# Chunk 1 of a Mamba-2 scan in two half-length units, and weight pieces joined one step later

## The chip, the cores and the metric

The kernel runs on one core of one Trainium2 chip. The metric is the device time of one execution in microseconds (us). The three runs of the kernel before gave 376.62, 376.66 and 376.97 us; their median, 376.66 us, is the time that the change is measured against. The profiled execution, from which all other times here come, spans 374.1 us.

## The reference, cut to what matters

```python
# batch 4, heads 8, sequence 768, head_dim 32, d_state 16; all float32
for c in range(nc):                                  # per head; state is [16, 32]
    cum = np.cumsum(log(clip(a[c])))                 # decay within the chunk
    L   = np.exp(cum[:, None] - cum[None, :]) * causal
    M   = (C @ B.T) * L
    y   = M @ x + (C @ state) * np.exp(cum)[:, None]
    state = exp(sum(la)) * state + (B * decay_to_end).T @ x
# then, with the heads side by side as 256 features, for 3072 tokens:
h = y @ w_in            # 256 -> 2048
g = h * np.cos(h)
out = g @ w_out         # 2048 -> 256
```

The result does not depend on the chunk length; the kernel chooses its own.

## The kernel before, in words

**Order of the work.** The sequence of 768 tokens is cut into six chunks of 128 tokens (`NC` = 6), for all four sequences together, so one chunk is 512 tokens. The feed-forward part of a chunk takes 16 steps (`NF` = 16), numbered through the whole kernel: steps 0 to 15 are chunk 0, 16 to 31 chunk 1, and so on up to 95. A step n consists of these parts, each on its engine, and each engine takes its instructions in the order in which the program writes them:

- `first(n)`, TensorE: eight matmuls (L668) make `hp`, 256 features of h for half of the chunk's tokens, in PSUM. `hp` has two banks, so `first(n)` needs the bank that step n-2 used.
- `wind(n)`: ScalarE makes k from `hp` (L675), VectorE makes w (L681).
- `gate(n)`: ScalarE takes the cosine (L690). `gated(n)`: VectorE multiplies `hp` with it into `gT` (L695), which frees the bank.
- `second(n-2)`, TensorE, two steps later (`LAG` = 2): `gT` times `w_out`. In chunk 0 that is eight matmuls of L739; from chunk 1 on it is a seven-product form (`seven`, L777), for which GpSimd prepares sums of `gT` in `differ` (L720 to L723) and sums of weights in `differ_w` (L714, in steps 14, 15, 17 and 19).

In chunk 0 a step takes the tokens of one *unit*: 64 tokens of every sequence (`turn_of`: even steps unit 0, odd steps unit 1, each two steps on the same 256 features). In the later chunks a step takes all 128 tokens of two sequences.

**Weights in pieces.** The weights come in as double words and have to be rounded to float32 on the chip. Each of `w_in` and `w_out` has eight pieces; piece j of either holds what the steps 2j and 2j+1 of a chunk use. `fetch` starts the load, `grade` takes the absolute value on ScalarE (L231), clips it on GpSimd (L232) and prepares the last bit on ScalarE (L229), and `join` builds the word on VectorE (L244, then L246) and adds the last bit on GpSimd (L254). `piece` (L886) says which piece belongs to which step: `out` j to step 2j, `in` j to step 2j-3. In the loop, step n grades the piece of step n+1 and joins the piece of step n; `join` stands after `wind(n)` and ahead of `gated(n)` in VectorE's queue. Pieces fetched but not joined hold one of eight `words` buffers.

**The scan.** Chunk 0 is scanned as two units of 64 tokens (`inner`, `weights`, `finish0`), with its decays spread over partitions by matmuls (`spread_a`) and scanned on VectorE by `decays0`. Chunk 1 is scanned as the later chunks are, one pair of sequences (u = 0, 1) at a time: `decays` scans a row of decays of 128 tokens of four heads (L515), eight times per chunk; `reaches` scans the decay from the chunk's start (L506); `turn2` turns B and C (for chunk 1 by four TensorE transposes, L543, later by VectorE, L529); `intra2` makes C times B (L565); `masked` multiplies it with the decays (L586, eight VectorE instructions per pair); `finish2` makes y and the state (L600, L607, L628) and `carry` sums the state (L640 on VectorE, L644 on GpSimd). `plan` (L892 to L899) says in which step which of it stands: for chunk 1, pair 0, the decays in steps 4, 6, 8 and 9, `turn2` in 11, `intra2` in 12 and `finish2` in 14; pair 1 in 14 to 17, 18, 19 and 21. VectorE does the decays behind `gated(n)` as long as there are pieces.

**Loads.** `rest_of_loads` (L906) writes the order of SyncE's DMA queue: chunk 1's data, sequence by sequence, between the remaining weight pieces.

Of the kernel before, what the change touches and what calls it, by code (L numbers as in the profile page):

```python
# [25 lines left out]
def kernel(  # L26
# [17 lines left out]
    P = 128  # L44
# [46 lines left out]
    def load(c, seqs=(0, NB), only=(B, C, x)):  # L91

        if c >= NC:
            return
        if c not in raw:
            raw[c] = (loads.tile([P, 2, NB * H, N], FP32, tag="bc", name="bc"),
                      loads.tile([P, NB, H, D], FP32, tag="xr", name="xr"))
        bc, xr = raw[c]
        xr = xr.rearrange("p b h d -> p (b h) d")
        for dst, src in ((bc[:, 0], B), (bc[:, 1], C), (xr, x))[::2 if c > 1 else 1]:  # L100

            if not any(src is o for o in only):
                continue
            halves = src is not C
            for b in range(*seqs) if halves else seqs[:1]:
                rs = slice(b * H, (b + 1 if halves else seqs[1]) * H)
                for t in range(2 if halves and b % 2 else 1):
                    n = W if halves and b % 2 else P
                    ts = slice((n - t * W) % P, (n - t * W) % P + n)
                    nc.sync.dma_start(  # L110
                        out=dst[ts, rs], in_=src[b:b + 1 if halves else seqs[1], :,
                                                 c * P + t * W:c * P + t * W + n, :]
                        .rearrange("b h s n -> s (b h) n"))
# [3 lines left out]
    both = loads.tile([P, 2, NB * H, N], FP32, tag="bc", name="bc")  # L117
    bs = both[:, 0].rearrange("p (k q h) n -> p k q (h n)", k=2, q=2)
    c4 = both[:, 1].rearrange("p (h r) n -> p h r n", h=H)
    xrs = {}  # L120

    def load_b(k, s, eng=nc.sync):

        eng.dma_start(out=bs[s * W:(s + 1) * W, k].rearrange("p q (h n) -> p (q h) n", h=H),
                      in_=B[2 * s:2 * s + 2, :, k * W:(k + 1) * W, :]
                      .rearrange("b h i n -> i (b h) n"))
# [7 lines left out]
    def load_x(k, s, eng=nc.sync):  # L134
        if k not in xrs:
            both = loads.tile([P, 2, 2, H, D], FP32, tag="xr", name="xr")
            xrs.update({i: both[:, i] for i in range(2)})
        eng.dma_start(out=xrs[k][s * W:(s + 1) * W].rearrange("p q h d -> p (q h) d"),
                      in_=x[2 * s:2 * s + 2, :, k * W:(k + 1) * W, :]
                      .rearrange("b h i d -> i (b h) d"))  # L140

    def by_blocks(c, u):
        return c > 1
# [22 lines left out]

    def load_along(c, seqs=range(NB)):

        if c >= NC:
            return  # L170
        if c not in along:
            along[c] = rows.tile([P, NB, P], FP32, tag="along", bufs=2, name="along")
        for b in seqs:
            nc.sync.dma_start(
                out=along[c][:, b], in_=a_all[b, :, c * P:(c + 1) * P].unsqueeze(1)
                .to_broadcast([H, N, P]))
# [8 lines left out]
                            .rearrange("p (b i) -> p b i", b=NB) for i in range(3))  # L185
    a_in = const.tile([RB, NU, P], FP32, name="a_in")
# [168 lines left out]
    def decays0(k, p, i=0, n=1):  # L355

        if p == i == 0:
            lams[k] = scan.tile([P, 2, H, W], FP32, tag="lam", bufs=4, name="lam")
        flat = "p h i -> p (h i)"
        hs = slice(i * H // n, (i + 1) * H // n)  # L360
        V.tensor_tensor_scan(out=lams[k][:, p, hs].rearrange(flat),
                             data0=spread.pop((k, p, i)).rearrange(flat),
                             data1=unit0[:, hs].rearrange(flat), initial=0.0,
                             op0=ALU.mult, op1=ALU.add)

    def weigh0(k):
        scs[k] = sc = scan.tile([P, 2 * H, N], FP32, tag="sc0", bufs=1, name="sc0")
        G.tensor_tensor(out=sc, in0=bs[:, k].rearrange("p q (h n) -> p (q h) n", h=H),
                        in1=lams[k].rearrange("p q h i -> p (q h) i")[:, :, W - 1:W]
                        .to_broadcast([P, 2 * H, N]), op=ALU.mult)  # L370
# [4 lines left out]
    bTs = scan.tile([P, 2, 2, P], FP32, tag="turned", bufs=1, name="turned0")  # L375
# [16 lines left out]
    def turn_b(k, tp):  # L392

        for p in range(2):
            PE.transpose(tp[:, 2 * k + p], bs[:, k, p], ident)
        return lambda: ACT.copy(out=bTs[:, k], in_=tp[:, 2 * k:2 * k + 2])
# [15 lines left out]

    def inner(k, t):

        gs[k, t] = g = pair("g")
        bT, cT = bTs[:, k], cuts[k]
        for p, s, q in ((p, s, q) for p in range(2) for s in range(2) for q in range(2)):
            ss, q_ = slice(s * W, (s + 1) * W), 2 * t + q
            r = slice(32 * q_, 32 * q_ + 32)
            PE.matmul(g[ss, q, p * P:(p + 1) * P].rearrange("p (t i) -> p t i", t=2),  # L420
                      lhsT=bT[r, p, ss], rhs=cT[r, :, p, ss], start=True, stop=True,
                      tile_position=(32 * q_, s * W), skip_group_check=True)

    def weights(k, q):

        m_of[k] = units[k]
        m, l = (ap[:, :, HH * q:HH * (q + 1)].rearrange("p s (k t) i -> p k s (t i)", k=2)
                for ap in (units[k], lams[k]))
# [3 lines left out]
    def finish0(k):  # L432

        m, xk = units[k], xrs[k]
# [31 lines left out]
        if k == 0:  # L466
            yT[0] = two.tile([P, 2, 2, 2 * P], FP32, tag="yT", name="yT")
        t_ = yT[0][:, k]
# [15 lines left out]
        def add():  # L484
            dec = scan.tile([P, 2, 2, 2 * D], FP32, tag="whole", bufs=1, name="whole")
            r4 = reach1.rearrange("p (q s) i -> p s q i", s=2)
# [4 lines left out]
            for u in range(2):  # L491
                state[0, u] = new[:, u].rearrange("p s (t d) -> p s t d", t=2)
# [40 lines left out]
    def turn2(c, u):  # L533
        bc = raw[c][0]

        if by_blocks(c, u):
            tp = turned.pop((c, u)).rearrange("p k s i -> p s k i")
            bT = tp[:, :, 0]
        else:
            tp = pair("tp")[:, 0].rearrange("p (s k i) -> p s k i", s=2, k=2)  # L540
            for s in range(2):
                for k in range(2):
                    PE.transpose(tp[:, s, k],  # L543
                                 bc[:, k, heads(2 * u + s)].rearrange("p h n -> p (h n)"), ident)
            bT = scan.tile([P, 2, 2, P], FP32, tag="turned", bufs=1, name="bT2")[:, 0]
            ACT.copy(out=bT, in_=tp[:, :, 0])
# [24 lines left out]
    def masked(c, b):  # L571
# [5 lines left out]
        if c == 1:  # L577
# [77 lines left out]
    def first(n, between=None, tag="h"):  # L655
# [4 lines left out]
        if c == 0:  # L660
            to_, y = hp[n].rearrange("p (e i) -> p e i", e=2), yT[0][:, u]
# [87 lines left out]
    def seven(n):  # L749
# [39 lines left out]
        def rest():  # L789
# [6 lines left out]
            for s in range(2):  # L796
                nc.sync.dma_start(out=to_rows[2 * u + s, c],
# [79 lines left out]
    def clips():  # L877
# [3 lines left out]
        for dst, src in ((a_cut, cut), (a_all, la)):  # L881
# [10 lines left out]
    late = [((0,), {0: 11}, [(4, 0, 0), (6, 0, 1), (8, 1, 0), (9, 1, 1)], 14),  # L892
            ((1,), {1: NF + 2}, [(NF - 2 + i, 2 + i // 2, i % 2) for i in range(4)], NF + 5)]
# [4 lines left out]
    plan = [(c, NF * (c - 1), *v) for c in range(1, NC) for v in (  # L898
        late if c == 1 else [(*at_once[:2], halves_of.get(c, each), at_once[2])])]  # L899

    def chunk1(b):
        load(1, (b, b + 1))
        load_along(1, (b,))
        load_a(1, (b,))

    def rest_of_loads():  # L906
        for w in (0, ("out", 3), ("in", 5), ("out", 4), 1,
                  ("in", 6), ("out", 5), ("in", 7), 2, ("out", 6), ("out", 7), 3):
            chunk1(w) if isinstance(w, int) else fetch(*w)
# [15 lines left out]
    def ends(n):  # L925
# [3 lines left out]
    block_loads = {NF * (c - 1) - 9 + 8 * u: (c, u) for c in range(2, NC) for u in range(2)  # L929
                   if by_blocks(c, u)}  # L930
# [3 lines left out]
    def first_steps():  # L934
# [3 lines left out]
        units_of_decay()  # L938
# [38 lines left out]
        join("in", 3)  # L977
        gated(3)
        grade("out", 2)
        return add_s1  # L980

    add_s1 = first_steps()
    rest_of_loads()
    for n in range(AHEAD, NC * NF + LAG):
        c, f = divmod(n, NF)
        if n < NC * NF:

            if c > 0 and f == (NJ if c == 1 else 0):
                if c == 1:
                    load(2, only=(x,))  # L990
                load(c + 2)
            first(n)
# [3 lines left out]
            rests = []  # L996
            if n + 1 in piece:
                rests.append(grade(*piece[n + 1], later=True))
            gate(n)
            for rest in rests:  # L1000
                if rest:
                    rest()
            if n in piece:
                join(*piece[n])

            behind = [lambda at=at: halved(*at) for at in halves_at(n)]
            behind = [lambda at=(c, 2 * u + 1): masked(*at) for c, u in pairs(n - 2)] + behind
            if n not in piece and behind:
                behind.pop(0)()
            gated(n)  # L1010
            if n == AHEAD + 2:
                add_s1()
            for do in (*behind, *unsummed):
                do()
            unsummed.clear()
        for i, js in differ_at.get(n, ()):
# [3 lines left out]
        for c, u in pairs(n - 1):  # L1020
            intra2(c, u)
            masked(c, 2 * u)
        for c, us in ends(n):
# [3 lines left out]
        for c, u in pairs(n + 1):  # L1027
# [3 lines left out]
            if by_blocks(c, u):  # L1031
                turn_blocks(c, u)
# [36 lines left out]
```

## Time and profile before

| what | us |
|---|---|
| median of three runs | 376.66 |
| span of the profiled execution | 374.1 |
| TensorE busy | 364.3 (97%) |
| VectorE busy | 282.7 (76%) |
| GpSimd busy | 216.1 (58%) |
| ScalarE busy | 172.1 (46%) |
| `hp` of step 4 starts | 27.16 |
| `hp` of step 24 starts | 106.67 |
| chunk 1's eight scans (L515), one each | 1.92, 1.92, 1.91, 1.92, 1.98, 1.22, 2.05, 1.42 |

In the page, a group is a line, an engine, an operation and its tiles with their shapes, then the number of instructions, the busy time and the mean of one. In a timeline, a line starts with the start and the duration of an instruction or of a merged run of them, and ends in brackets with the time for which the engine stood idle before it and what ended that. TensorE's granted clock is 1.0 throughout. A TensorE instruction of float32 counts twice in the profile (eight matmuls of `first(n)` for the four in the code). TensorE's busy share is no measure of its pace, since matmuls overlap: the distance between the starts of `hp` in two steps is.

### The profile page before, as it was taken

To read this page: it belongs to the slowest core of one execution; us is meant where nothing else is said; L and a number is where in the kernel's file an instruction comes from. 1 tells how busy PE (TensorE), PEld (TensorE's weight loads), DVE (VectorE), ACT (ScalarE), POOL (GpSimd) and SP (SyncE) were. 2 spreads that over 40 slices of the span, in tenths; PEclk is the share of its full clock that TensorE was granted. 3 is DMA by queue.
4 is the path that set the end of the run, shared out by engine and by line. 5 is a ranking of instruction groups with operands and counts; after the bars stand their busy time and mean duration, and the time that the engine had idled before them with its cause. 6 is when DMAs were issued, how large, how long until landed. Compare 5 with 4: busy or idle time off the path is not lost.

```text
span 374.1 us, 8667 instructions
## 1 busy us (share of the span) xinstructions
PE 364.3 (97%) x3262; PEld 326.9 (87%) x3262; DVE 282.7 (76%) x473; ACT 172.1 (46%) x293; POOL 216.1 (58%) x334
## 2 busy tenths in 40 slices
PE   8998999999999999999999999999999999999996
PEld 5687777889899899999899998999999989999995
DVE  7788999989699957987867987766887872554543
ACT  3586756444344434354434435434444443443442
POOL 6667765589946346665454693453785344544451
PEclk9999999999999999999999999999999999999999
DMA  9969797514545742653222745221020000010011
GB/s 147 283 180 257 206 255 127 128 14 97 140 106 76 133 95 31 88 151 93 59 54 22 133 99 135 28 45 17 3 41 8 13 18 2 2 28 0 2 31 29
DMA packets 121354, 31.55 MB, mean 84 GB/s; under 512 B 90496, under 2 KB 117216, under 8 KB 121312
## 3 DMA queue, kind: packets, MB, share of 16 engines
q1 hardware_dynamic: 119024, 30.54, 38.3%
q10 hardware_dynamic: 2288, 0.46, 0.7%
q8 instruction: 26, 0.43, 0.5%
q14 instruction: 16, 0.13, 0.1%
HBM read 27.64 MB, written 3.34 MB: 83 GB/s over the span
## 4 chain that ended last, share of the span: by engine, by line
PE 64%; DVE 13%; SPq 7%; POOL 7%; issue 4%; ACT 2%; DMA 2%; DVEq 0%; POOLq 0%; ACTq 0%
PE hp L668 30%; PE o L777 25%; SPq L155 4%; POOL words L714 3%; DVE gT L695 2%; DVE w L681 2%; PE y L607 2%; SPq L110 2%; DVE mag L246 2%; DVE lam L515 2%; DVE mag L244 2%; DMA arow<-a_cut 1%; PE y L600 1%; PE g L565 1%; PE a_ps L351 1%
## 5 line engine op out<-in xcount | busy, mean ns | idle before, releaser
L668 PE MATMUL hp<-yT,w_in 128*128 128x256 f32 x768 | 183.5, 382 | 3.2 <-DVE gT L695 2.9
L668 PEld LDWEIGHTS hp<-yT,w_in 128*128 128x128 f32 x768 | 139.3, 190 | 23.8 <-issue 5.7
L720 POOL TENSOR_TENSOR gd<-gT 128x256 f32<-128x256 f32 x79 | 59.0, 747 | 99.1 <-DVE gT L695 97.2
L690 ACT ACTIVATE w<-w,quarter 128x512 f32<-128x512 f32 x96 | 69.2, 721 | 80.2 <-DVE w L681 80.1
L681 DVE SCALAR_TENSOR_TENSOR w<-hp,k 128x512 f32<-128x512 f32 x96 | 65.5, 682 | 40.4 <-ACT k L675 40.2
L675 ACT ACTIVATE k<-hp 128x512 int32<-128x512 f32 x96 | 57.1, 595 | 79.7 <-PE hp L668 79.5
L695 DVE TENSOR_TENSOR gT<-hp,w 128x512 f32<-128x512 f32 x96 | 65.2, 680 | 33.2 <-ACT w L690 24.3
L777 PE MATMUL o<-words,gd 128*128 128x128 f32 x474 | 65.9, 275 | 0.0
L777 PEld LDWEIGHTS o<-words,gd 128*128 128x128 f32 x474 | 59.3, 192 | 0.0
L515 DVE TENSOR_TENSOR_SCAN lam<-arow,unit 128x512 f32<-128x512 f32 x40 | 56.5, 1411 | 0.0
L777 PEld LDWEIGHTS o<-w_out,gT 128*128 128x128 f32 x316 | 47.6, 191 | 3.9
L723 POOL TENSOR_TENSOR gd<-gT,gd 128x128 f32<-128x128 f32 x79 | 44.6, 565 | 6.2
L777 PE MATMUL o<-w_out,gT 128*128 128x128 f32 x316 | 48.0, 275 | 0.0
L722 POOL TENSOR_TENSOR gd<-gT,gd 128x128 f32<-128x128 f32 x79 | 44.1, 558 | 6.2
L586 DVE TENSOR_TENSOR m<-g,lam 128x256 f32<-128x256 f32 x80 | 30.9, 414 | 0.5
L739 PE MATMUL o<-w_out,gT 128*128 128x256 f32 x128 | 30.2, 380 | 0.4 <-POOL w_out L254 0.4
L777 PE MATMUL o<-w_out,gd 128*128 128x128 f32 x158 | 30.6, 275 | 0.0
L777 PE MATMUL o<-words,gT 128*128 128x128 f32 x158 | 30.6, 275 | 0.0
L739 PEld LDWEIGHTS o<-w_out,gT 128*128 128x128 f32 x128 | 24.2, 190 | 4.0 <-POOL w_out L254 0.8
L777 PEld LDWEIGHTS o<-words,gT 128*128 128x128 f32 x158 | 24.0, 192 | 0.0
L777 PEld LDWEIGHTS o<-w_out,gd 128*128 128x128 f32 x158 | 24.0, 192 | 0.0
L794 DVE TENSOR_TENSOR sum<-ps,sum 128x256 f32<-128x256 f32 (+1 forms) x27 | 16.7, 644 | 0.6
(109 smaller groups left out, 269.5 us busy)
## 6 DMA issues: line engine op xcount, KB each, us to landing
arow<-a_cut SPq DMA_DIRECT2D x20, 512.0 KB
words<-in_moe_w_in_dram SPq DMA_DIRECT2D x8, 512.0 KB
words<-in_moe_w_out_dram SPq DMA_DIRECT2D x8, 512.0 KB
out_dram<-sum SPq DMA_DIRECT2D x18, 128.0 KB
blocks<-in_B_dram SPq DMA_DIRECT2D x128, 8.0 KB
blocks<-in_C_dram SPq DMA_DIRECT2D x128, 8.0 KB
xr<-in_x_dram SPq DMA_DIRECT2D x14, 128.0 KB
along<-a_all SPq DMA_DIRECT2D x20, 64.0 KB
```

The source lines that it names most:

```text
L515: V.tensor_tensor_scan(out=lam[c, b][:, hs].rearrange("p h i -> p (h i)"), data0=rows_.rearrange("p h i -> p (h i)"), data1=unit[:, b % 2 ...
L586: V.tensor_tensor(out=m_[js, :, :, is_], in0=g_[js, :, :, is_], in1=l_[js, :, :, is_], op=ALU.mult)
L668: PE.matmul(to_[:, e], lhsT=w_in[:, k, fs], rhs=y[:, k], start=(k == 0), stop=(k == KT - 1), skip_group_check=True)
L675: ACT.activation(k, hp[n], AF.Copy, bias=0.25, scale=INV_2PI)
L681: V.scalar_tensor_tensor(out=w, in0=hp[n], scalar=INV_2PI, in1=k, op0=ALU.mult, op1=ALU.subtract)
L690: ACT.activation(cos, cos, AF.Sin, bias=quarter, scale=TWO_PI)
L695: V.tensor_tensor(out=gT[n], in0=hp.pop(n), in1=cos, op=ALU.mult)
L720: G.tensor_tensor(out=d[:, 0:2], in0=g[:, 1:2].to_broadcast([P, 2, P]), in1=g[:, 3::-3], op=ALU.subtract)
L722: G.tensor_tensor(out=d[:, 2], in0=g[:, 0], in1=d[:, 0], op=ALU.subtract)
L723: G.tensor_tensor(out=d[:, 3], in0=g[:, 2], in1=d[:, 2], op=ALU.subtract)
L739: PE.matmul(o[c, u][:, t], lhsT=g[:, 2 * e + t], rhs=w_out[:, 2 * j + e], start=(j == e == t == 0), stop=(j == NJ - 1 and e == 1), skip_gr ...
L777: PE.matmul(at[q], lhsT=a_[q], rhs=w[q], start=(j == 0 and q in starts), stop=(j == NJ - 1), skip_group_check=True)
```

## The change

Chunk 1 is scanned as chunk 0 is: in two units, here numbered k = 2 and 3, each 64 tokens of all four sequences. It is for less work on VectorE: a scan of 64-token rows covers twice as many (sequence, head) pairs per instruction, and half of a 128x128 causal square is not computed at all. The second part moves `join` one step behind `grade`, so that a piece's clip lies a whole step ahead of the join.

```diff
-        if by_blocks(c, u):
-            ...
-        else:
-            tp = pair("tp")[:, 0].rearrange("p (s k i) -> p s k i", s=2, k=2)
-            ...
-                    PE.transpose(tp[:, s, k], ...)
+    def load_arow(k):            # two loads of [W, 2H, W] per unit
+    def load_unit_along(k):      # four loads of [H*N, W] per unit
...
+    def reach_unit(k):           # one VectorE scan of 128x260
+    def turn_unit(k):            # 4 transposes, ACT: bT, 2 x cT; VectorE: rT
...
-            if n + 1 in piece:
-                rests.append(grade(*piece[n + 1], later=True))
+            rest = grade(*piece[n], later=True) if n in piece else None
             gate(n)
...
-            if n in piece:
-                join(*piece[n])
+            joins = n - 1 in piece and piece[n - 1] in held
+            if joins:
+                join(*piece[n - 1])
...
+    unit_at = {2: ((6, 8), 9, 11, 12, 14),
+               3: ((NF - 1, NF), NF + 1, NF + 2, NF + 3, NF + 5)}
...
         gate(3)
         rest()
         second(1)
-        join("in", 3)
         gated(3)
-        grade("out", 2)
...
-        if c == 1:
+        if c == 2:
 
             G.memset(m[W - s * W:P - s * W, :, 0:W], 0.0)
```

`unit_at` gives for each unit the steps of the two decay scans (`decays0`), of `reach_unit`, of `turn_unit`, of `inner` with the first half of `weights` (the second half follows a step later), and of `finish0`; the state's sum (`add`, three GpSimd instructions, L488 and L490) follows a step after `finish0`. `units_of_decay`, two GpSimd copies (L873, L875), moves from the first steps to the end of step 16, behind `weigh0(3)`. The memsets of the mask tiles (L579) move from chunk 1 to chunk 2. `rest_of_loads` is written anew in the order of the units, with chunk 2's first rows of decays loaded in steps 12 and 17; the shapes of `first`, `seven` and the output of chunk 1 follow the units.

## The prediction

> **What bounds the kernel now.** I read the page's busy shares first, then the busy time in stretches of 10 us, then the timelines of TensorE and VectorE through chunk 0, where the change acts. The stretches (sums of busy time of PE, PEld, DVE, ACT, POOL in us) show two regimes:
>
> ```profile
> 40.00:50.00 10.00, 9.82 (x46) 8.36 (x45) 9.90 (x13) 7.29 (x13) 8.62 (x11) 1.00 0.91 249
> 50.00:60.00 10.00, 9.29 (x45) 7.58 (x44) 9.93 (x13) 5.80 (x12) 6.06 (x6) 1.00 0.80 199
> ...
> 200.00:210.00 10.00, 10.00 (x70) 9.39 (x69) 7.92 (x11) 4.94 (x9) 7.55 (x12) 1.00 0.44 49
> ```
>
> From 200 us TensorE sets the pace: weight loads fill 94%, and `hp` starts every 3.29 us. From 40 to 60 us VectorE is full (99%) and TensorE has gaps. The PE timeline names their ends:
>
> ```profile
> 29.59 2.00 PE L739 MATMUL o<-w_out,gT 128*128 128x256 f32 x8 [0.43 <-POOL w_out L254]
> 31.42 1.89 PE L668 MATMUL hp<-yT,w_in 128*128 128x256 f32 x8
> 33.15 1.89 PE L739 MATMUL o<-w_out,gT 128*128 128x256 f32 x8
> 35.64 1.96 PE L668 MATMUL hp<-yT,w_in 128*128 128x256 f32 x8 [0.61 <-DVE gT L695]
> ```
>
> Eight matmuls follow each other in 1.73 us (31.42 to 33.15), so a chunk-0 step can take 2 x 1.73 = 3.46. The starts P of `hp` (L668 in this view): step 4 27.16, 5 31.42, 7 39.72, 9 47.04, 11 54.51, 13 63.48, 15 72.42, 17 79.43, 24 106.67. From step 4 to 17 that is 52.27 us. TensorE's own work is 13 x 3.46 = 44.98, transposes 0.54, `intra2` 0.84, `finish2` 1.83: 48.19. So 4.1 us are lost there, mostly to `gT` coming late and freeing `hp` late. Later, 79.43 to 106.67, about 0.7 us is lost (0.35 of it a wait for the memset of L579 at 98.61). That is the whole prize.
>
> **What the skill says.** "SBUF — State Buffer", section "Who interferes with whom": a VectorE instruction with two SBUF inputs and a GpSimd instruction that reads SBUF exclude one another, and so does a VectorE instruction in a two-port mode; the second waits. The trace agrees (a line of GpSimd's timeline, then one of VectorE's):
>
> ```profile
> 41.89 1.27 POOL L254 TENSOR_TENSOR w_out<-mag,last 128x512 uint32<-128x512 uint32 x1 [0.63 <-DVE mag L246]
> ...
> 42.33 1.92 DVE L515 TENSOR_TENSOR_SCAN lam<-arow,unit 128x512 f32<-128x512 f32 x1
> ```
>
> The scan starts inside the GpSimd add and ends 1.09 us after it; undisturbed ones take 1.22. "TensorE: Matmul & The Clock Gate", section "Step-by-step: what each phase is for": only weight loads are pulled ahead, matmuls stay in program order. The line at 29.59 agrees: `second(2)` waits for its weights and `hp` of the next step waits behind it.
>
> **The change, part by part.**
>
> *VectorE, removed.* For chunk 1: eight scans (14.4 us by their durations), four of L506 (2.4), two rT (0.8), sixteen mask products (16 x 0.414 = 6.6), four `carry` sums (1.1): 25.3. *Added:* four scans (1.22 to 1.92, so 4.9 to 7.7), two `reach_unit` (0.67 each, the row L403 of 128x260), two rT (0.8), four `weights` (0.69 each, row L429, 2.7): 9.7 to 12.5. About 14 us less, 9 of them in steps 4 to 14. VectorE then has some 28 us of work where TensorE needs 38, and `gT` no longer sets the pace. This mechanism I expect to work.
>
> *The join, moved.* This is where I expect the gain to go. `out` j (step 2j) is now joined in step 2j+1, behind w(2j+1) in VectorE's queue, and `second(2j)`, which reads it, stands in step 2j+2 right behind `first(2j+2)`. Before, it had a step more. The chain in an unhurried step, from P(2j+1): k starts 1.98 later and w 0.63 after k (step 16: `hp` 75.98, k 77.96, w 78.59); from w to the end of the GpSimd add 3.19, as step 14 shows (VectorE's timeline, the last line GpSimd's):
>
> ```profile
> 70.26 0.69 DVE L681 SCALAR_TENSOR_TENSOR w<-hp,k 128x512 f32<-128x512 f32 x1
> 70.86 0.42 DVE L244 TENSOR_SCALAR mag<-mag 128x512 uint32<-128x512 uint32 x1
> 71.32 0.71 DVE L246 SCALAR_TENSOR_TENSOR mag<-words,mag 128x512 uint32<-128x512 uint32 x1
> ...
> 72.18 1.27 POOL L254 TENSOR_TENSOR w_out<-mag,last 128x512 uint32<-128x512 uint32 x1 [4.20 <-DVE mag L246]
> ```
>
> That ends at 73.45. With 0.05 to TensorE (29.54 to 29.59), `second(2j)` can start at P + 1.98 + 0.63 + 3.19 + 0.05 = P + 5.85. At TensorE's pace it would start at P + 3.46 + 1.73 = P + 5.19. Behind it in TensorE's queue stand `first(2j+3)` and everything after, so the 0.66 is lost each time, for `out` 2 to 7: six times. Restarting costs about 0.07 (35.64 to 37.44 is 1.80, not 1.73). A pair of steps then takes 5.85 + 1.80 = 7.65 at least.
>
> On top: the clip of the step's own piece (L232, 0.61) is ready for GpSimd at k + 0.48 + 0.68 + 0.1 = k + 1.26, and L244 starts at k + 0.63 + 0.60 = k + 1.23: they exclude each other. Where they met before, either L244 took 0.82 to 0.85 in place of 0.42 (33.34, 56.70) or L246 0.98 in place of 0.69 (40.83): 0.3 to 0.4. I take 0.3 for the four odd steps with a piece to clip (5, 7, 9, 11), 1.2 in all; the bounds are 0 and 1.7. Step 7 meets the state sums (L488, L490) of step 6, 0.2; step 11 has rT (0.33) ahead of its join. The `in` pieces, joined in even steps for `first(n+2)`, are ready at P + 5.85 against P + 6.92 and cost nothing. Sum from step 5 to 17: 6 x 7.65 = 45.9, + 1.2 + 0.2 + 0.3, + 0.8 for `inner` and 1.75 for `finish0`, whose transposes hide in the wait: 50.2. Before: 79.43 - 31.42 = 48.0. So **2.2 us slower** by step 17.
>
> *First steps.* Steps 4 and 5 start as before, since `in` 2 and `out` 1 are still joined there (27.16, 29.59). `join("in", 3)` leaves the path of gT(3), so `hp` of step 6 starts 0.7 earlier (35.64 to 34.9), which the 7.65 already holds.
>
> *TensorE.* `inner` (32 instructions of L420 took 0.72 at 8.52) for `intra2` (0.84), `finish0` (L445, L454, L462: about 1.7) for `finish2` (1.83): 0.2 less per unit.
>
> *GpSimd.* Per unit `weigh0` 0.64 and `add` 2.6 (rows L368, L488, L490) for two memsets, two L498 and one L644: 0.7 more each. `units_of_decay`, 1.5 by its two rows, moves into step 16, where GpSimd is full (95% from 80 to 100 us) and `differ(16)` to `differ(18)` are due. But `differ_w` of step 14 no longer stands behind a join that waits for VectorE (the 4.20 above), which gives more than 1.5 back. I take nothing, and keep 1 us for the range. The memsets in chunk 2 lie beside GpSimd's idle time.
>
> *ScalarE and SyncE.* ScalarE gets some 0.7 us per unit at 46% busy; nothing waits. The rows of decays come as half as many bytes and the weight pieces earlier; the only wait on a load in these steps (0.8 us for `out` 3 at 35.65) goes, since it is graded a step later. Off the path: nothing.
>
> *Steps 17 to 24:* the memset's 0.35 and 0.3 of TensorE work: 0.65 less. From step 24 TensorE sets the pace as before.
>
> Sum: + 2.2 - 0.65 = + 1.6, with the clip's clash not everywhere + 1.3: **378.0 us**.
>
> **The rivals.**
>
> *A: the joins are hidden, and relief of VectorE is the whole story.* For it: VectorE's 99%, and the 9 us taken off it. Against it: the chain of P + 5.85, which has no slack in it. If two thirds of the 4.1 + 0.7 us lost are won, 2.7: 374.0. Chance 0.25.
>
> *B: a draw.* Without the clash the sum is 48.5 against 48.0, less 0.65: 376.5; a wait for `w_out` takes the place of the wait for `gT`. Chance 0.2.
>
> *C: GpSimd becomes the bound in steps 16 to 20* by `units_of_decay` and the sums, on top of the late joins. For it: the second product of `second(18)` needs `differ` at 93.1, whose L722 ends at 92.75. Another 1.3: 379.3. Chance 0.12.
>
> **How the numbers follow.** The late joins, alone, have 0.43, at 378.0; with C that makes slower 0.55; same 0.2 (B); faster 0.25 (A). Ends: A reaches down to 372 if everything is won; 374.2 leaves out less than half of it. The clash at its upper bound and C give 379.6, with little beyond.
>
> **What would show it.** In the profile after: the idle time of L739 in steps 6, 8, 10, 12, 14 and 16, released by GpSimd's L254, 0.6 to 1 us each; gT no more a releaser of L668 in steps 6 to 13; VectorE well under 99% from 40 to 60 us; P of step 17 near 81.6, of step 24 near 108.2. Wrong if L739 never waits, which would mean that w or the join starts earlier in the step than step 14 shows; or if P of step 17 lies before 79, or L777 waits on L722 after step 18.

## The result, and the profile after

The changed kernel takes 380.16 us (median of 18 runs, 379.56 to 384.17) beside 377.28 us for the kernel before in the same runs: a ratio of 1.0079, with an interval of 1.0054 to 1.0104. That is 2.9 us slower, more than twice the 1.3 us forecast, and half a microsecond above the top of the range. An execution more than 1.5% above the fastest of its kernel counts as slow, and the ratios are taken from the others, which leaves out two of the six of experiment 1, the profiled one among them, and three of the 22 of experiment 3. The execution that the profile of the change shows took 384.17 us, with a wait in step 43 that, going by their times, is shorter or absent in most (16 of the 18 took 381.51 us or less). So the two profiles are compared step by step, and the medians for the whole.

The stretches of 10 us of the changed kernel, with the columns of the prediction's first fence, show that the relief of VectorE came:

```profile
40.00:50.00 10.00, 8.81 (x41) 7.45 (x40) 8.86 (x10) 5.52 (x10) 7.88 (x9) 1.00 0.91 222
50.00:60.00 10.00, 9.29 (x45) 7.86 (x45) 7.93 (x13) 7.03 (x15) 4.87 (x6) 1.00 0.90 159
```

VectorE (third column) falls from 99% to 89% and 79%. But TensorE (first column) is no fuller than before: 8.81 for 9.82 in the first stretch. Its timeline names what it waits for instead:

```profile
34.70 1.89 PE L705 MATMUL hp<-yT,w_in 128*128 128x256 f32 x8
37.25 1.99 PE L776 MATMUL o<-w_out,gT 128*128 128x256 f32 x8 [0.65 <-POOL w_out L278]
...
45.61 1.99 PE L776 MATMUL o<-w_out,gT 128*128 128x256 f32 x8 [1.19 <-POOL w_out L278]
...
53.50 1.99 PE L776 MATMUL o<-w_out,gT 128*128 128x256 f32 x8 [0.71 <-POOL w_out L278]
...
62.13 1.99 PE L776 MATMUL o<-w_out,gT 128*128 128x256 f32 x8 [1.02 <-POOL w_out L278]
...
70.64 1.99 PE L776 MATMUL o<-w_out,gT 128*128 128x256 f32 x8 [0.49 <-POOL w_out L278]
...
80.31 1.99 PE L776 MATMUL o<-w_out,gT 128*128 128x256 f32 x8 [0.49 <-POOL w_out L278]
...
91.89 0.94 PE L814 MATMUL o<-words,gd 128*128 128x128 f32 x6 [0.23 <-POOL gd L759]
...
97.02 0.94 PE L814 MATMUL o<-words,gd 128*128 128x128 f32 x6 [0.73 <-POOL gd L759]
```

(L705, L776, L814 and L278 are here what L668, L739, L777 and L254 are before. In the lines below, L256, L268 and L270 are L232, L244 and L246; L535 and L537 are L488 and L490; L751 and L759 are L714 and L722.) `gT` releases no `hp` any more in steps 6 to 13; six times it is the joined `w_out` that `second` waits for, 4.55 us in all. The last two lines are new: the seven-product form in steps 19 and 20, `second(17)` and `second(18)`, waits for GpSimd's `differ`.

The chain that makes `w_out` late is seen in step 5, whose `hp` starts at 31.25. VectorE's timeline, and then GpSimd's:

```profile
33.81 0.69 DVE L718 SCALAR_TENSOR_TENSOR w<-hp,k 128x512 f32<-128x512 f32 x1 [0.18 <-ACT k L712]
34.41 0.41 DVE L268 TENSOR_SCALAR mag<-mag 128x512 uint32<-128x512 uint32 x1
34.86 0.98 DVE L270 SCALAR_TENSOR_TENSOR mag<-words,mag 128x512 uint32<-128x512 uint32 x1
```

```profile
34.43 0.88 POOL L256 TENSOR_SCALAR mag<-mag 128x512 f32<-128x512 f32 x1
35.93 1.26 POOL L278 TENSOR_TENSOR w_out<-mag,last 128x512 uint32<-128x512 uint32 x1 [0.62 <-DVE mag L270]
...
78.99 1.27 POOL L278 TENSOR_TENSOR w_out<-mag,last 128x512 uint32<-128x512 uint32 x1 [4.41 <-DVE mag L270]
80.22 1.68 POOL L535 TENSOR_TENSOR whole<-state,m 128x128 f32<-128x128 f32 x2
81.98 1.60 POOL L537 TENSOR_TENSOR state<-state,whole 128x256 f32<-128x256 f32 x1
83.54 2.62 POOL L751 TENSOR_TENSOR words<-w_out,words 128x512 f32<-128x512 f32 x2
```

From `hp` to `w_out` ready it is 37.19 - 31.25 = 5.94 us, where TensorE, at its pace, would have been ready after 5.19. The clip of the step's own piece (34.43) falls on top of the join, and the two are longer together than apart, 0.98 us for 0.69 and 0.88 for 0.61. From 78.99 on GpSimd is seen in a queue of its own: the last join waits 4.41 us for VectorE, the state's sum and `differ_w` (L751) come after it, and behind them `differ(16)` to `differ(18)`.

Third, step 43, which the prediction didn't look at (TensorE's timeline):

```profile
189.93 1.03 PE L602 MATMUL g<-cT,turned 32*64 32x256 f32 x32 [2.90 <-ACT cT L586]
191.43 3.23 PE L705 MATMUL hp<-yT,w_in 128*128 128x256 f32 x8 [0.47 <-DVE gT L732]
```

`intra2` of chunk 3's second pair waits 2.90 us, and the eight matmuls behind it take 3.23 us instead of 1.89. (This `intra2` stands in step 44, behind the `turn2` of step 43; the wait is called that of step 43 throughout.)

The starts of `hp` put sizes to it, in the two profiles, and in two later experiments (9 and 10), which are the same two kernels with some loads moved, so that nothing waits in step 43:

| steps | forecast | after less before | 9 less 10 |
|---|---|---|---|
| 5 to 17 | +2.2 | 50.89 - 48.01 = +2.88 | 51.05 - 47.99 = +3.06 |
| 17 to 24 | -0.65 | 27.91 - 27.24 = +0.67 | 28.04 - 27.24 = +0.80 |
| 24 to 29 | 0 | 19.52 - 19.12 = +0.40 | 19.51 - 19.12 = +0.39 |
| 29 to 43 | 0 | 50.72 - 50.72 = 0 | 50.72 - 50.72 = 0 |
| 43 to 95 | 0 | 191.52 - 187.02 = +4.50 | 186.74 - 186.75 = 0 |

### The profile page after: what moved, and what is told of

Its sections match the earlier page's. It is cut to its first block, busy times and chain, and to the rows that moved or that the text cites. A ratio compares the mean times of both kernels' runs of the same rounds, so it can differ in the third digit from the quotient of the medians.

```text
span 382.4 us, 8913 instructions
## 1 busy us (share of the span) xinstructions
PE 366.3 (96%) x3390; PEld 327.8 (86%) x3390; DVE 272.4 (71%) x451; ACT 173.7 (45%) x299; POOL 219.1 (57%) x339
## 2 busy tenths in 40 slices
DMA packets 121835, 30.51 MB, mean 80 GB/s; under 512 B 95584, under 2 KB 117696, under 8 KB 121792
## 4 chain that ended last, share of the span: by engine, by line
PE 70%; SPq 8%; POOL 8%; DVE 5%; issue 4%; DMA 3%; ACT 3%; DVEq 0%; ACTq 0%; POOLq 0%
PE hp L705 32%; PE o L814 25%; SPq L153 5%; PE o L776 3%; PE y L644 2%; POOL w_out L278 2%; POOL words L751 2%; DVE mag L270 2%; DMA arow<-a_cut 1%; PE a_ps L375 1%; PE y L637 1%; DVE mag L268 1%; ACT k L712 1%; SPq L109 1%; POOL whole L535 1%
## 5 line engine op out<-in xcount | busy, mean ns | idle before, releaser
L705 PE MATMUL hp<-yT,w_in 128*128 128x256 f32 x768 | 184.4, 384 | 1.7 <-DVE gT L732 1.3
L705 PEld LDWEIGHTS hp<-yT,w_in 128*128 128x128 f32 x768 | 140.5, 191 | 21.2 <-PE g L602 1.9
L757 POOL TENSOR_TENSOR gd<-gT 128x256 f32<-128x256 f32 x79 | 60.1, 760 | 100.2 <-DVE gT L732 98.7
L814 PE MATMUL o<-words,gd 128*128 128x128 f32 x474 | 66.0, 275 | 1.0 <-POOL gd L759 1.0
L814 PEld LDWEIGHTS o<-words,gd 128*128 128x128 f32 x474 | 59.2, 192 | 1.3 <-POOL gd L759 1.3
L814 PEld LDWEIGHTS o<-w_out,gT 128*128 128x128 f32 x316 | 47.4, 191 | 4.1 <-ACT ps L823 0.2
L814 PE MATMUL o<-w_out,gT 128*128 128x128 f32 x316 | 48.0, 275 | 0.0
L759 POOL TENSOR_TENSOR gd<-gT,gd 128x128 f32<-128x128 f32 x79 | 43.6, 553 | 6.2
L562 DVE TENSOR_TENSOR_SCAN lam<-arow,unit 128x512 f32<-128x512 f32 x32 | 42.9, 1341 | 0.0
L776 PE MATMUL o<-w_out,gT 128*128 128x256 f32 x128 | 30.8, 385 | 5.0 <-POOL w_out L278 5.0
L776 PEld LDWEIGHTS o<-w_out,gT 128*128 128x128 f32 x128 | 23.7, 190 | 10.7 <-POOL w_out L278 7.8
L814 PE MATMUL o<-w_out,gd 128*128 128x128 f32 x158 | 30.6, 275 | 0.0
L814 PE MATMUL o<-words,gT 128*128 128x128 f32 x158 | 30.5, 275 | 0.0
L623 DVE TENSOR_TENSOR m<-g,lam 128x256 f32<-128x256 f32 x64 | 24.7, 415 | 0.4
L814 PEld LDWEIGHTS o<-w_out,gd 128*128 128x128 f32 x158 | 24.0, 192 | 0.0
L814 PEld LDWEIGHTS o<-words,gT 128*128 128x128 f32 x158 | 24.0, 192 | 0.0
L278 POOL TENSOR_TENSOR w_out<-mag,last 128x512 uint32<-128x512 uint32 x8 | 10.1, 1267 | 13.3 <-DVE mag L270 13.3
```

The source lines that it names most:

```text
L562: V.tensor_tensor_scan(out=lam[c, b][:, hs].rearrange("p h i -> p (h i)"), data0=rows_.rearrange("p h i -> p (h i)"), data1=unit[:, b % 2 ...
L623: V.tensor_tensor(out=m_[js, :, :, is_], in0=g_[js, :, :, is_], in1=l_[js, :, :, is_], op=ALU.mult)
L705: PE.matmul(to_[:, e], lhsT=w_in[:, k, fs], rhs=y[:, k], start=(k == 0), stop=(k == KT - 1), skip_group_check=True)
L757: G.tensor_tensor(out=d[:, 0:2], in0=g[:, 1:2].to_broadcast([P, 2, P]), in1=g[:, 3::-3], op=ALU.subtract)
L759: G.tensor_tensor(out=d[:, 2], in0=g[:, 0], in1=d[:, 0], op=ALU.subtract)
L776: PE.matmul(o[c, u][:, t], lhsT=g[:, 2 * e + t], rhs=w_out[:, 2 * j + e], start=(j == e == t == 0), stop=(j == NJ - 1 and e == 1), skip_gr ...
```

## The experiments

One correction first. The description of the change says that the second part puts "a whole step" between a piece's clip and its join. In the loop of the kernel before, that step was there already: step n graded the piece of step n+1 and joined that of step n. The change moves both one step later (except for `in` 3 and `out` 2 in the first steps, which were closer). The prediction's working had the right steps.

**The two parts apart.** Theory: the units win time, and the late joins lose more than that. Rivals: the units are worth nothing once `gT` is early, or the loss is GpSimd's.

Experiment 1 keeps the units and puts grade and join back where they were:

```diff
+        join("in", 3)
         gated(3)
+        grade("out", 2)
...
-            rest = grade(*piece[n], later=True) if n in piece else None
+            rest = grade(*piece[n + 1], later=True) if n + 1 in piece else None
...
-            joins = n - 1 in piece and piece[n - 1] in held
+            joins = n in piece and piece[n] in held
             if joins:
-                join(*piece[n - 1])
+                join(*piece[n])
```

> The units of the change, with the pieces of weights graded and joined in the steps of the kernel before. Theory (the joins moved a step later cost the time): TensorE waits for no w_out behind step 4, the start of hp of step 17 lies 45 to 46.5 us behind that of step 5 (48.0 before, 50.9 after), and the kernel is 2 to 3 us faster than before, ratio about 0.993. GpSimd's lateness in steps 16 to 20 shrinks too, since the join of the last piece no longer stands in step 15. Rival (the units themselves cost the time): it stays at the changed kernel's ratio of 1.008.

It took 385.16 us (median of 6 runs, 380.02 to 389.27; the profiled execution 387.85), ratio 1.0147 (1.0088 to 1.0205) where 0.993 was expected: no faster than the change, and by the median slower. Yet the early part went as the theory has it. No `second` waits for `w_out` from step 6 on, steps 5 to 17 take 45.70 us (before 48.01) and 17 to 24 take 26.54 (27.24): 3.0 us won by step 24. All is lost again in two places, the second of them step 43 (TensorE's timeline of experiment 1):

```profile
123.42 0.91 PE L602 MATMUL g<-cT,turned 32*64 32x256 f32 x32 [1.87 <-ACT cT L586]
...
193.49 1.59 PE L602 MATMUL g<-cT,turned 32*64 32x256 f32 x32 [10.83 <-ACT cT L586]
195.00 3.35 PE L705 MATMUL hp<-yT,w_in 128*128 128x256 f32 x8
```

The profile names ScalarE's cT; what cT is made from is VectorE's transposes, and VectorE's timeline leads on to a load:

```profile
185.40 0.45 DVE L576 STREAM_TRANSPOSE turned<-blocks 128x256 f32<-128x256 f32 x1 [4.33 <-DMA blocks<-in_B_dram]
...
192.05 0.45 DVE L576 STREAM_TRANSPOSE turned<-blocks 128x256 f32<-128x256 f32 x1 [6.21 <-DMA blocks<-in_C_dram]
```

(The shorter wait at 123.42 is of the same kind: the transpose ahead of it waits 1.67 us for a block.) The load is late because it was issued late. SyncE issues all loads in the order in which the program writes them, at 0.6 to 0.8 us each in the rows below, and in its queue's timeline one row follows the other almost without a gap. Experiment 1, and then the kernel before with VectorE's transpose:

```profile
159.81 3.78 SPq L109 DMA_DIRECT2D bc<-in_B_dram  x6
163.69 4.77 SPq L109 DMA_DIRECT2D xr<-in_x_dram  x6
...
187.95 2.46 SPq L153 DMA_DIRECT2D blocks<-in_C_dram  x4
```

```profile
176.24 1.24 SPq L174 DMA_DIRECT2D along<-a_all  x2
177.53 2.39 SPq L155 DMA_DIRECT2D blocks<-in_C_dram  x4
...
181.48 0.45 DVE L529 STREAM_TRANSPOSE turned<-blocks 128x256 f32<-128x256 f32 x1 [0.15 <-issue]
```

The last block of chunk 3 is issued at 187.95 to 190.41, when TensorE has long been in step 43 (from 175.91). Before, it was issued at 177.53 to 179.92, and the transpose ran at 181.48: just in time in the profiled execution. "Perfetto Trace Analysis", section "What 'DMA-bound' means", names this as a bound of its own, an issuing engine's sequencer track that is solid DMA slices, and says that such a track is not data movement. The trace agrees: from 180 to 190 us of experiment 1 the DMA engines are 51% busy. In the four runs that the ratio counts, TensorE's mean granted clock is 0.986 to 0.990, beside 0.986 in the profiled one, where the pause lowers it (see the last section); that speaks for a like pause in them, but no profile shows it.

Experiment 2 is the other half: the late joins on the kernel before, which keeps its pairs.

```diff
-        join("in", 3)
         gated(3)
-        grade("out", 2)
...
-            if n + 1 in piece:
-                rests.append(grade(*piece[n + 1], later=True))
+            rest = grade(*piece[n], later=True) if n in piece else None
...
-            if n in piece:
-                join(*piece[n])
+            joins = n - 1 in piece and piece[n - 1] in held
+            if joins:
+                join(*piece[n - 1])
```

> The kernel before with nothing changed but the steps in which pieces are graded and joined, as in the change. Theory: w comes later in the step here, since VectorE is full, so second waits for w_out longer than in the changed kernel: 52 to 53 us from step 5 to 17 in place of 48.0, ratio 1.010 to 1.013. Rival (the late join is harmless, the units cost): ratio 1.000.

380.73 us (11 runs, 380.11 to 382.43), ratio 1.0072 (1.0046 to 1.0098): the late joins alone cost as much as the whole change, though less than the 1.010 to 1.013 expected. The six waits are there, in TensorE's timeline (three of them, with the others 0.71, 1.11 and 0.52):

```profile
38.44 1.99 PE L739 MATMUL o<-w_out,gT 128*128 128x256 f32 x8 [1.94 <-POOL w_out L254]
...
46.50 1.99 PE L739 MATMUL o<-w_out,gT 128*128 128x256 f32 x8 [0.88 <-POOL w_out L254]
...
81.53 1.99 PE L739 MATMUL o<-w_out,gT 128*128 128x256 f32 x8 [0.49 <-POOL w_out L254]
```

Steps 5 to 17 take 52.19 us, as expected, 4.2 more than before. Step 43 has no wait: TensorE reaches it 4.1 us later than before (180.62), and the last block is issued from 179.46 on.

**The clash of clip and join.** Experiment 3 is the changed kernel with the clip behind the join:

```diff
-            rest = grade(*piece[n], later=True) if n in piece else None
             gate(n)
-            if rest:
-                rest()
...
             if joins:
                 join(*piece[n - 1])
+            if n in piece:
+                grade(*piece[n])
```

> The changed kernel with grade behind join in each step, so that GpSimd clips behind the join's add and VectorE's two instructions of the join meet no clip. Theory (the clash of clip and join is some 0.3 us of each wait for w_out in steps 6 to 12): L270 takes 0.69 in place of 0.98, the waits shrink by 0.3 four times, 1.2 us in all, ratio to before about 1.0047. Rival (the clash is hidden or moves elsewhere): ratio stays at 1.008.

380.16 us (22 runs), ratio 1.0070 (1.0045 to 1.0094), not to be told from the change; 1.0047 was expected. The edit does remove the clash: L270 takes 0.69 us in the joins of steps 5, 9 and 11 (in step 7, where something else meets it, 1.10 with and without the edit). Yet the six waits sum to 4.21 us for 4.55, and steps 5 to 17 take 50.68 for 50.89. In step 5 the chain from `hp` to `w_out` even grows, from 5.94 to 6.11 us, because the piece's own clip, now behind the join of the step before, ends at 34.59 and L268 can start only at 34.63. So taking the clash away is worth about 0.2 us by this edit, and not 1.2.

**GpSimd's queue in steps 15 to 20.** In the changed kernel the state's sum (L535, L537) runs between the last join and `differ_w`. Experiment 4 puts the sum of unit 2 out of the way, from step 15 into step 20 (that of unit 3 stays in step 22):

```diff
-            if add_s and (n == AHEAD + 2 or units_at(n - 1, 4)):
+            if add_s and n in (AHEAD + 2, NF + 4, NF + 6):
                 add_s()
```

> The changed kernel with the state sum of unit 2 (three GpSimd instructions) in step 20 in place of step 15. Theory (the sum, 3.3 us between the last join and differ_w, is what makes GpSimd late in steps 17 and 18): L814's waits for L759 (0.23 and 0.73 us) vanish, 1.0 to 1.2 us less, ratio to before about 1.005. Rival (the last join, now in step 15, makes GpSimd late by itself, or the copies of units_of_decay do): the waits stay, ratio 1.008.

385.06 us (6 runs), ratio 1.0180 (1.0146 to 1.0214), where 1.005 was expected. The two waits of L814 are gone, though the last join still waits 4.46 us. In experiment 1 they are absent too, with the sum in step 15 and the join a step earlier. So it takes both, the late join and the sum behind it. But the state is now late for its reader, as TensorE's timeline shows:

```profile
105.07 1.23 PE L492 MATMUL y<-rT,state 32*64 32x64 f32 x32 [4.69 <-POOL state L537]
```

The cause of the two waits is settled by the two runs; a gain is not to be had by moving the sum as far as this.

**The issue queue.** New theory: SyncE's queue sets step 43, in experiment 1 fully, in the change a little, and in the kernel before at times. Rival: the wait is the transfer's own time. The first try takes a part of the issues off SyncE: every second block load of chunks 2 and 3 is issued on ScalarE.

```diff
+                        eng = nc.scalar if h and c < 4 else nc.sync
-                        nc.sync.dma_start(out=to_[...], in_=of[m, h])
+                        eng.dma_start(out=to_[...], in_=of[m, h])
```

Experiment 5 does so to experiment 1, 6 to the change, 7 to the kernel before.

> Experiment e1 (units, with the joins in the steps of the kernel before) with half of the small B and C loads of chunks 2 and 3 issued on ScalarE's queue in place of SyncE's. Theory (e1's early gain is given back in step 43, where TensorE waited 10.8 us for blocks of chunk 3 that SyncE's queue issued late): the blocks arrive 10 us or more earlier, the wait goes, the clock stays at 1.0, and the gain of steps 5 to 17 stays: 373 to 375 us, ratio 0.990 to 0.994. Rival (the DMA engines, not the queue, are late, or the units lose elsewhere): a wait of some us stays in step 43, ratio 1.0 or more.

> The changed kernel with the same half of the loads on ScalarE's queue. Theory (in the changed kernel the late joins and GpSimd have cost 3.5 us by step 24, and the late blocks cost little beyond that, since TensorE comes late to step 43 itself): hp of step 17 and 24 stay where they were, the waits in step 43 (0.3 to 2.9 us) go, ratio to before 1.004 to 1.007. Rival (the loads are the whole loss): ratio 0.995 to 1.000.

> The kernel before with the same half of the loads on ScalarE's queue. Theory (in the kernel before the blocks of step 43 come just in time, 0.3 us late): 0 to 0.5 us faster, ratio 0.999 to 1.000. Rival (loads of chunk 2 and 3 held the kernel before, too): 2 us faster or more, ratio 0.995.

| | us (6 runs each) | ratio |
|---|---|---|
| 5: units, early joins | 382.49 | 1.0101 (1.0064 to 1.0137) |
| 6: units, late joins | 384.69 | 1.0164 (1.0127 to 1.0200) |
| 7: pairs, early joins | 384.04 | 1.0151 (1.0117 to 1.0186) |

What was expected of the times missed: the kernel before lost 5.9 us by the edit. The 64 issues take ScalarE's queue 0.56 us each on average, 36 us in all, and experiment 5 shows new waits on what ScalarE makes (1.27 us for `ob` at 84.75, 0.89 for cT at 127.73). "DMA: Bandwidth & Descriptors", section "Issuing engines are not separate DMA queues", says that issuing on several engines only saves the sequencer's time to initiate, "which is usually small relative to the DMA itself". Here that time is what there is to save, and on ScalarE, at 0.56 us an issue, it is taken from work that others wait for. Still, the wait of step 43 went in experiment 5, and between kernels with the same edit the order is the theory's: by the medians, units with early joins are 1.6 us faster than pairs with early joins, and late joins cost the units 2.2 us (the intervals of the ratios overlap).

The second try leaves the issues on SyncE and changes their order: eighteen loads of chunks 3 and 4 which nobody needs so soon are written behind the last blocks of chunk 3. (The twelve of chunk 5 move too, from step 48 to step 55.)

```diff
-            if c > 0 and f == (NJ if c == 1 else 0):
-                if c == 1:
-                    load(2, only=(x,))
+            if c == 1 and f == NJ:
+                load(2, only=(x,))
+                load(3, only=(B,))
+            if c > 1 and f == 7:
+                if c == 2:
+                    load(3, only=(x,))
                 load(c + 2)
```

Experiment 8 is experiment 1 with it, 9 the change, 10 the kernel before.

> Experiment e1 (units, joins in the steps of the kernel before) with the 18 loads of x of chunk 3 and of B and x of chunk 4 moved in SyncE's queue from ahead of the last blocks of chunk 3 to behind them; no engine gets or loses an instruction. Theory (SyncE's queue, full from 25 to 190 us, sets when step 43 can go on): the blocks come some 12 us earlier, the wait of 10.8 us in step 43 goes, the waits in steps 27 and 28 (1.9 and 0.9 us) stay, hp of step 45 starts near 183.5 us (184.4 before), ratio 0.996 to 0.999. Rival (the DMA engines are late whatever the order): a wait of several us stays in step 43, ratio above 1.005.

> The changed kernel with the same reordering of SyncE's queue. Theory (late joins and GpSimd cost 3.5 us by step 24, and the queue's lateness lies under that and shows only in some executions): hp of step 24 stays near 110, the waits in step 43 go, ratio 1.004 to 1.007. Rival (the queue is the changed kernel's whole loss): ratio 1.000 or less.

> The kernel before with the same reordering. Theory (its blocks come just in time): the wait of 0.3 us in step 43 goes and little else, ratio 0.998 to 1.000. Rival (nothing of the kernel before waited for the queue, and moving the loads makes others late): ratio above 1.002.

| | us | runs | ratio |
|---|---|---|---|
| 8: units, early joins | 373.33 (372.65 to 374.03) | 6 | 0.9871 (0.9840 to 0.9902) |
| 9: units, late joins | 379.95 (379.31 to 380.88) | 22 | 1.0049 (1.0033 to 1.0066) |
| 10: pairs, early joins | 375.84 (375.49 to 376.25) | 9 | 0.9934 (0.9909 to 0.9960) |

In experiment 8 the last blocks of chunk 3 are issued at 171.34, the loads that stood ahead of them come after, and VectorE transposes without a wait. SyncE's queue, then VectorE:

```profile
171.34 2.31 SPq L153 DMA_DIRECT2D blocks<-in_C_dram  x4
173.75 3.77 SPq L109 DMA_DIRECT2D xr<-in_x_dram  x6
177.62 4.57 SPq L109 DMA_DIRECT2D bc<-in_B_dram  x6
```

```profile
178.38 0.74 DVE L576 STREAM_TRANSPOSE turned<-blocks 128x256 f32<-128x256 f32 x2
```

The wait of 10.83 us is gone, and the same transfers in another order take 2.7% off experiment 1 (0.9871 / 1.0147 = 0.9728): the position in the queue was the cause, not the transfer. In the profiles 1.6 us of this are not the edit's: the wait in step 28, behind the `turn2` of step 27, is 0.29 us here for 1.87, and its blocks stand in the queue ahead of everything that was moved. Experiment 9 came out as expected. Experiment 8 is faster than the 0.996 to 0.999 expected of it, and experiment 10 says why. That is the one that surprised: the kernel before gains 0.66% too, and its runs, which spread over 375.9 to 380.4 us without the edit, draw together within 0.8 us. Of the 30 runs without the edit, 27 took longer than the slowest with it. So the kernel before lost some 2.2 us in its median execution (378.02 less 375.84) to this queue, though its profiled execution shows 0.3 us of it (187.02 for 186.75 in steps 43 to 95). That the loss lies in step 43 as it does in the change is likely, but not seen in a profile: of the eleven slowest of the 30, from 379.13 us on, ten show a mean granted clock of 0.994 or 0.995, as the change's profiled execution does (0.995), and all others 0.998 or more.

With the queue out of the way the two parts can be weighed. Units: 8 over 10, 0.9871 / 0.9934 = 0.9937, or 2.4 us won. Late joins: 9 over 8, 1.0049 / 0.9871 = 1.018, or 6.7 us lost. Together 1.0116, or 4.3 us, which agrees with the sum of the last column of the table of steps (4.24). The measured 1.0079 is smaller because the reordering is worth 0.66% to the kernel before and only 0.30% to the change: 1.4 us of the loss were hidden in a wait that the kernel before had anyway. The two parts don't simply add, though. On pairs the late joins cost 4.4 us by step 24 (79.61 us from step 5 to 24 in experiment 2, 75.25 before); on units it is 6.8 (79.09 in experiment 9, 72.26 in experiment 8), since there they also undo what the units have won. With late joins the units are worth only 0.8 us by step 24 (78.80 in the change), with early joins 3.0.

Experiment 11 is experiment 8 with the output of chunk 0 issued on ScalarE:

```diff
-            nc.sync.dma_start(out=unit_rows[p, u], in_=ob[p * W:(p + 1) * W])
+            nc.scalar.dma_start(out=unit_rows[p, u], in_=ob[p * W:(p + 1) * W])
```

> Experiment e8 with the four writes of chunk 0's output issued on ScalarE's queue, behind the copies that they write, in place of SyncE's, where they stand ahead of the blocks of chunk 2's second pair. Theory (the wait of step 27 is the same lateness of SyncE's queue): the blocks of step 27 come 3 to 5 us earlier, the wait of 1.9 us goes, hp of step 45 starts near 181.5, ratio 0.991 to 0.995. Rival (the write on ScalarE delays k, or other loads become late): ratio as e8 or above.

372.98 us (6 runs, 372.83 to 373.69), ratio 0.9868 (0.9835 to 0.9901), not to be told from experiment 8. The last blocks for step 27 are issued 3.4 us earlier (111.98 for 115.35) and their wait is gone, as expected, but in experiment 8 it was down to 0.29 us already. (The ratio is below the 0.991 to 0.995 expected, for the same reason as in experiment 8.) Both beat the two kernels of this case: by about 5 us the kernel before, by about 7 the change.

## Why the prediction was right in its direction and wrong in its size

*VectorE's relief: right.* `gT` no longer releases `hp` in steps 6 to 13, and experiment 1 shows what that is worth when the joins stay: 2.3 us in steps 5 to 17. VectorE's busy time fell by 10.3 us (282.7 to 272.4), where about 14 were reckoned. The relief was said to be real and to be swallowed, and it was. The sign that was named for it came too: L739 (here L776) waits in steps 6 to 16, every second one, 0.49 to 1.19 us each.

*"A pair of steps then takes 5.85 + 1.80 = 7.65 at least": right.* The pairs from step 5 on took 7.83, 8.36, 7.89, 9.37, 9.68 and 7.76 us; the forecast, with its additions, was 7.95, 8.15, 7.95, 9.08, 9.40 and 7.65. Each is within 0.3, and the sum 0.7 short (50.2 for 50.89). The terms that were too small are those for steps 7, 11 and 13, where more than one thing lies ahead of the join. The contention that "SBUF — State Buffer" describes in "Who interferes with whom" was met as forecast where the clip lies on the join, 0.29 us on L270; but little of it reaches the end, 0.2 us by experiment 3 for the 1.2 reckoned. So the 0.3 us then taken off the sum, "with the clip's clash not everywhere", was right of the clash; that the sum as a whole needed more and not less comes from the other terms.

*"GpSimd ... I take nothing": this step failed.* The argument was that `differ_w` no longer stands behind a join that waits for VectorE, and that this "gives more than 1.5 back". For the `differ_w` of step 14 that held (it starts at 72.07, before at 73.41). But the wait of 4.20 us in step 14 became one of 4.41 in step 15, since the join that had moved is the same join, and it is the `differ_w` of step 15 that now stands behind it (83.54, before 78.89). Between the two came the state's sum, 3.3 us where the rows gave 2.6. `units_of_decay`, which was feared, took 0.83 and not 1.5. So steps 17 to 24 cost 0.67 to 0.80 us instead of winning 0.65; 0.96 of the difference are the two waits of L814, and experiments 1 and 4 show the late join and the sum together as their cause. "L777 waits on L722 after step 18", a sign of being wrong by the prediction's own list, came true in steps 19 and 20. For the units alone the -0.65 was right: experiment 1 has 26.54 for 27.24, -0.70. This is rival C, and the second error lies in how it was set: it was given 0.12 as an alternative at 379.3, when it is a consequence of the likeliest case and comes on top of it.

*"From step 24 TensorE sets the pace as before": 0.4 us short.* At the start of chunk 2 the wait for `gT` grew from 0.65 to 0.86 us and `intra2` came later by 0.15. It comes with the units: experiment 2, which has none, takes 19.12 us here as the kernel before does. In the change GpSimd sums the state of unit 3 from 110.39 to 112.03 (L535 and L537), and beside it VectorE's rT and scan take 0.63 and 1.75 us, where in experiment 2 they take 0.40 and 1.21. That this sets the later `gT` is read from the traces and wasn't tried.

*"ScalarE and SyncE ... Off the path: nothing": this step failed, but it is not what made the change slow.* The bytes fell from 31.55 to 30.51 MB, and the working stopped there. What counts on SyncE is the time that its issues take, and their place: the last block of chunk 3 is issued at 184.30 in the change and at 179.46 in experiment 2, which has the same late joins without the units. Up to the end of this block the queue holds 245 issues in either (four more of decays in the change, four fewer of B, C and x), but they take 163.5 us for 158.1. Why they take longer isn't shown. The transfers themselves may have a part in it: from 45 to 65 us, with the DMA engines 88% busy, an issue of the change takes 1.09 us on average, and from 100 to 190 us, with 50%, 0.58. In the change most of that delay is hidden, since TensorE itself comes to step 43 3.8 us later than before. In experiment 1, where TensorE comes early, it took back everything.

*The baseline.* The median of the kernel before already held a loss to the queue, 0.8 us of it in the 376.66 us forecast from (375.84 without it). The profile that was read was of one that had lost next to nothing, and a single execution doesn't show that a load arrives with nothing to spare; the row that would have told it is the transpose at 181.48, 1.6 us behind the end of the issue of its load.

The sum, then: forecast 2.2 - 0.65 = 1.6, taken 1.3. Happened: 3.06 + 0.80 + 0.39 = 4.25, less 1.4 hidden in the queue's wait, 2.9. That the miss was no larger is luck: a wait that the prediction didn't know of hid a third of the loss.

Three of its sums don't come out as written. The clash at its upper bound (0.5 more than the 1.2 taken) and C (1.3), added to the 1.6, give 380.1 and not the 379.6 where the range ended; from the 1.3, 379.8. B's 48.5 leaves out all that was added for clashes, sums and rT, 1.7 us; without the clash alone it is 49.0, and B 377.0. And A's 2.7 us are two thirds of 4.1; of the 4.1 + 0.7 named they would be 3.2.

## What to carry to other kernels

A consumer on the busiest engine sets how late a preparation may come: reckon the chain from the step's start to the last instruction of the preparation, with everything that shares its queues, against the moment at which the consumer would be ready, before moving it later. When an operation with a long wait moves, its wait moves with it, and so does what stands behind it in the queue. And look along the DMA issue queue for loads that land just when they are needed: a kernel made faster ahead of such a load gets nothing, and the order of the issues can be worth more than the change.

## What the runs showed of the hardware that wasn't expected

After a long pause TensorE itself ran slower. In experiment 1 the windows of the profile (busy time of the five engines, then the granted clock, the DMA share and GB/s) read:

```profile
190.00:194.00 4.00, 0.51 (x17) 0.52 (x25) 1.35 (x3) 1.47 (x4) 0.00 (x0) 0.50 0.17 17
194.00:200.00 6.00, 6.00 (x53) 4.87 (x41) 4.21 (x9) 2.04 (x5) 3.27 (x6) 0.69 0.27 48
200.00:210.00 10.00, 10.00 (x173) 9.23 (x172) 5.18 (x13) 3.58 (x7) 4.10 (x8) 1.00 0.20 31
```

The pause of 10.83 us ends at 193.49; the clock is halved when the matmuls start again and whole from 200 us on; eight matmuls took 3.35 us for 1.89. "TensorE: Matmul & The Clock Gate", section "What's actually happening", has it so: an idle window of about 3.4 us halves the clock, and about as long a busy one restores it. In the change a wait of 2.90 us, shorter than that, was already enough (3.23 us for eight matmuls), and in experiment 2 one of 1.94 us was not: the eight matmuls behind it started 1.83 us before the next. These are two cases and no threshold. By the first, a pause of some 3 us in this kernel costs about 1.3 us beyond its own length (3.23 - 1.89, an estimate).

The other is the price of an issue: some 0.58 us of SyncE's queue for a block load (2.31 us for four), so that fewer bytes in as many issues are no relief, and some 6 us of the kernel's time when every second block load of two chunks went to ScalarE.
